# Output stores merged per tile and put on SyncE's queue, part of a weight block transposed in bf16, and a new order of all steps

## The chip, the core and the metric

The kernel runs on one core of one Trainium2 chip. The core has a matrix engine (TensorE, PE in the profile; its weight loads are shown as PEld), a vector engine (VectorE, DVE), a scalar engine (ScalarE, ACT), GpSimd (POOL) and SyncE (SP), each with its own queue of instructions that are carried out in order. SyncE does no arithmetic here, it issues transfers. ScalarE and GpSimd can issue transfers too. All transfers are moved by the same 16 DMA engines.

The metric is device time in microseconds of one execution.

## What is computed

A linear attention over 8 batches, 8 heads, 576 positions and 64 numbers per head, followed by a multiplicative feed-forward step on the 4608 tokens of width 512:

```python
phi(x) = where(x > 0, x, exp(x) - 1) + 1
kv  = einsum('bhsd,bhse->bhde', phi(k), v)
z   = sum(phi(k), axis=2)
num = einsum('bhsd,bhde->bhse', phi(q), kv)
den = einsum('bhsd,bhd->bhs', phi(q), z)[..., None] + 1e-06
x   = (num / den) with the heads side by side      # 4608 x 512
out = ((x @ w1) * (x @ w2)) @ w3 @ w_out           # w1, w2: 512 x 1024; w3: 1024 x 1024; w_out: 1024 x 512
```

Inputs and output are float32. The kernel forms w3 @ w_out once (it is called wf, 1024 x 512), so that each token needs x @ w1, x @ w2, their product, and one product with wf.

## The kernel before

**An order written out.** The program is the string ORDER, a list of steps such as `F.2.0` or `VC.3.0.v`. Each step is a small function `s_<kind>`; the letter at the end says which engine does its copy (a ScalarE, v VectorE, p GpSimd, s SyncE). The steps are recorded in this order, and each engine's queue holds its part of them in this order. An engine that waits at one instruction holds up all later ones of its queue.

**Loads.** All loads go through `load` (L150) on SyncE's queue into one of 13 buffers called `ld`: L3.i a block of 128 rows of w3, LO.x two blocks of w_out, LA.x and LB.x a quarter of w1 and w2 (256 columns), LQ/LK/LV.b.h half of q, k, v of batch b (576 KB). A load waits until the last reader of its buffer is done.

**The product wf.** T3.i transposes the eight 128 x 128 parts of block i of w3 in float32 on TensorE (L198) into a PSUM tile of two banks and copies it to bf16 (L201). CO casts w_out to bf16 (L179). FA.i (L209) and FB.i (L213) are four matmuls each of w3's block with w_out; FB copies the result to wf (L214). CA and CB cast the quarters of w1 and w2 (L183, L188).

**Attention.** EX is the exponential on ScalarE (L222), PT and PM are phi's other two parts on VectorE (L234, L241), VC casts v to bf16 (L244). KV.b.h is 36 small matmuls for half a batch's kv (L260) and a copy (L262). q is transposed on TensorE for batches 0 and 1 (QP, L273 and L274) and by a transposing transfer on SyncE's queue for the others (QD, L278). ND.t forms numerator and denominator of the 128 tokens of tile t (L292) and divides on VectorE (L298 to L300) into xn. A tile holds two sets of 64 tokens; a set is one batch b and one j of 9, with 64 tokens that stand 9 rows apart in the output, and tile t has sets 2t and 2t+1. Four tiles make a chunk of 512 tokens. xn is transposed on TensorE for chunks 0 and 1 (XP, L314 and L315) and by transposing transfers for the others, two tiles each (XD, L319).

**Feed-forward.** F.c.f is eight matmuls of 128 x 512 for chunk c and 128 columns f of w1 and w2 (L337), a copy of one product to SBUF on ScalarE (L343) and the multiplication on VectorE (L344). O.t is eight matmuls of the products with wf (L359) and a copy to o_sb (L366), which has five buffers. Four PSUM banks (`mm`) are shared by F, O, XP, FA and the warm-up; two tiles of two banks (`at`) by ND, KV, QP and T3.

**Stores.** S.t sends o_sb to HBM in two transfers of 64 rows on GpSimd's queue (L375). Q.35 is the last tile: two halves of 256 columns, each copied and stored on its own, on SyncE's and ScalarE's queues (L382, L385).

Of the kernel before, what the change touches and what calls it, by code (L numbers as in the profile page):

```python
# [14 lines left out]
P = 128  # L15
# [3 lines left out]


ORDER = """
L3.1 I.0 H.9 I.1 L3.0 T3.0.a T3.1.v LO.0 L3.2 T3.2.a CO.0.v LO.1 CO.1.v FA.1 FA.0 LO.2 CO.2.v FA.2
LO.3 CO.3.v FB.1.a L3.3 L3.5 FB.0.v L3.4 LQ.0.0 LQ.0.1 T3.3.v FB.2.v PT.q.0.1 PT.q.0.0 T3.4.a T3.5.a
EX.q.0.0 L3.6 LV.0.0 FA.3 PM.q.0.0 FA.4 EX.q.0.1 PM.q.0.1 FB.3.a I.2 T3.6.a LK.0.0 LK.0.1 VC.0.0.v
L3.7 LV.0.1 PT.k.0.0 EX.k.0.0 FA.5 LA.0 QP.0.1.v QP.0.0.a PM.k.0.0 EX.k.0.1 LQ.1.1 FB.4.a LB.0 FA.6
KV.0.0.a T3.7.a FB.5.a LA.3 PT.k.0.1 PM.k.0.1 LB.1 LA.1 VC.0.1.v KV.0.1.a ND.0 ND.1 CA.0.a FB.6.a
ND.2 XP.0.a LA.2 EX.q.1.1 ND.3 FA.7 XP.1.a XP.2.v XP.3.v FB.7.v CA.3.v CB.0.a PT.q.1.1 LK.1.0
PM.q.1.1 F.0.0 CB.1.v CA.1.a F.0.1 F.0.2 CA.2.a PT.k.1.0 LB.2 CB.2.v LQ.1.0 EX.k.1.0 PM.k.1.0 LB.3
LV.1.0 PT.q.1.0 F.0.3 F.0.4 EX.q.1.0 QP.1.1.v CB.3.a F.0.5 VC.1.0.a F.0.6 LK.1.1 PT.k.1.1 LV.1.1
EX.k.1.1 PM.k.1.1 KV.1.0.a PM.q.1.0 VC.1.1.a LQ.5.1 F.0.7 KV.1.1.a QP.1.0.a LQ.2.1 O.0.a LK.3.0 ND.4  # L30
ND.5 O.1.a LK.2.0 PT.k.2.0 EX.k.2.0 LV.2.0 XP.4.v XP.5.v EX.q.2.1 ND.6 ND.7 LK.2.1 O.2.v XP.6.a
EX.k.3.0 PT.k.3.0 XP.7.v VC.2.0.v LQ.2.0 PT.q.2.0 LV.3.0 LV.2.1 LQ.3.1 LV.4.1 LQ.3.0 PM.k.2.0 O.3.a
LK.4.1 EX.q.2.0 LK.4.0 PT.k.2.1 F.1.0 F.1.1 PT.q.2.1 PM.q.2.1 F.1.2 EX.k.2.1 PM.k.3.0 F.1.3 PT.q.3.1
# [25 lines left out]
def kernel(  # L59
# [61 lines left out]
    def at_tile(name):  # L121
        return take("at", name, [P, 2, 512], F32, name)
# [24 lines left out]
    def load(key, src, cols):  # L147
        t = raw[key] = take("ld", key, [P, HW], F32, key[0])[:, 0:cols]
        dst = t if len(src.shape) == 2 else t.rearrange("p (a x) -> p a x", a=src.shape[1])
        nc.sync.dma_start(out=dst, in_=src)  # L150
# [26 lines left out]

    def s_CO(x, e):
# [1 line left out]
        give("ld", ("wo", x))  # L180

    def s_CA(x, e):
        copy_of(e)(out=w1_sb[:, :, 256 * x:256 * x + 256],  # L183
                   in_=raw["wa", x].rearrange("p (c n) -> p c n", c=KC))
        give("ld", ("wa", x))

    def s_CB(x, e):
        copy_of(e)(out=w2_sb[:, :, 256 * x:256 * x + 256],  # L188
                   in_=raw["wb", x].rearrange("p (c n) -> p c n", c=KC))
        give("ld", ("wb", x))  # L190


    w3ts = {}

    def s_T3(i, e):
        tp = at_tile("w3p").rearrange("p a (c t) -> p (a c) t", t=P)
        for c in range(FC):
            nc.tensor.transpose(tp[:, c, :], raw["w3", i][:, c * P:(c + 1) * P], ident32)  # L198
# [12 lines left out]
    def s_FB(i, e):
        for c in range(4, 8):
            nc.tensor.matmul(wfs[i], w3ts[i][:, c, :], wo_sb[:, c, :], start=False, stop=(c == 7))  # L213
        copy_of(e)(out=wf_sb[:, i, :], in_=wfs[i])  # L214
        give("mm", ("wf", i))
# [35 lines left out]
    def s_KV(b, h, e):
        if h == 0:
            kvs[b] = take("kv", None, [P, 2, 2, E], BF16, "kv")
        kvp = at_tile("kvp")
        kh = by_set("k", phs["k", b, h])
        for j in range(J):
            for c in range(2):
                for u in range(2):
                    rows = slice(u * R, (u + 1) * R)
                    nc.tensor.matmul(kvp[c * R:(c + 1) * R, u, 0:E], kh[rows, c, j, :],  # L260
                                     vts[b % 2][rows, h, c, j, :], start=(j == 0), stop=(j == J - 1))
        copy_of(e)(out=kvs[b][:, h], in_=kvp[:, :, 0:E])  # L262
        give("at", "kvp")

    def q_tile(b, h):
# [100 lines left out]
        copy_of(e)(out=o_sbs[t], in_=o_ps)  # L366
# [59 lines left out]
```

## Time and profile before

| | |
|---|---|
| three executions | 259.6, 259.3 and 258.11 us, median 259.3 |
| the profiled execution | 259.34 us; its span from the first to the last instruction is 257.6 us |
| mean granted TensorE clock | 0.979 |
| TensorE busy | 235.3 us, 91% of the span |
| VectorE, ScalarE, GpSimd busy | 156.7 us, 116.2 us, 39.9 us |
| transfers | 55.79 MB, 217 GB/s on average |
| first F (F.0.0) starts | 36.75 us |
| last O's matmuls start | 249.75 us |

The matrix engine's busy time counts from the start of a matmul to its modelled end, so it does not say how fast the matmuls run; the granted clock does that. In a group of the profile, "x72 | 49.1, 686" means 72 instructions, 49.1 us in all, 686 ns each; what follows the next bar is the time that the engine stood idle ahead of them, and what ended it. "SPq" is SyncE's queue. A DMA share of 1.0 means that all 16 engines had packets all the time, and it can be above 1 where packets of two queues overlap.

### The profile page before, as it was taken

The page shows a single profiled execution, that of the slowest core. Times are in us where ns is not written, and L with a number is a line of the kernel's source. Part 1 is how long each engine was busy: PE and PEld are TensorE (multiplying, and loading weights), DVE is VectorE, ACT ScalarE, POOL GpSimd, SP SyncE. Part 2 cuts the span into 40 slices and gives each one's busy share as a digit, 9 for nine tenths or more (in the row PEclk, how much of TensorE's full clock was granted, in tenths as well). Part 3 has the DMA queues.
Part 4 walks back from the last instruction along what each step waited for, and adds up shares of the span by engine and source line. Part 5 has one row for each costly group of instructions (what it writes and reads, how often), then busy time and mean ns, then how long its engine had stood idle before and what let it go on. Part 6 is the DMA issues. An engine that isn't in the chain of part 4 may idle for free.

```text
span 257.6 us, 5461 instructions
## 1 busy us (share of the span) xinstructions
PE 235.3 (91%) x2206; PEld 114.2 (44%) x2229; DVE 156.7 (61%) x294; ACT 116.2 (45%) x165; POOL 39.9 (15%) x79
## 2 busy tenths in 40 slices
PE   6799689999999698999996999999999999999990
PEld 2465444454445343444443444444444444444450
DVE  0448588769898748897988359534557215424420
ACT  1328777957584247346555443235323232231310
POOL 2000000014101600050031101033201330132140
PEclk9999999999999979999999799999999999999996
DMA  6999999999999999799999923653714431331232
GB/s 246 394 401 396 368 356 370 390 390 403 400 267 288 331 320 299 146 204 233 370 187 267 294 45 59 160 106 83 150 43 83 91 73 41 81 84 25 57 85 78
DMA packets 52216, 55.79 MB, mean 217 GB/s; under 512 B 31264, under 2 KB 35616, under 8 KB 52192
## 3 DMA queue, kind: packets, MB, share of 16 engines
q1 hardware_dynamic: 48672, 46.15, 61.0%
q0 software_dynamic: 3360, 9.18, 14.0%
q8 instruction: 17, 0.28, 0.5%
q10 hardware_dynamic: 160, 0.13, 0.2%
q14 instruction: 7, 0.06, 0.1%
HBM read 38.80 MB, written 9.44 MB: 187 GB/s over the span
## 4 chain that ended last, share of the span: by engine, by line
PE 68%; DMA 17%; DVE 6%; SPq 3%; issue 2%; ACT 1%; DVEq 0%
PE a_ps L337 22%; PE b_ps L337 22%; PE o_ps L359 20%; DMA k<-in_k_dram 5%; DMA v<-in_v_dram 5%; DMA w<-in_moe_w_dram 4%; DMA q<-in_q_dram 3%; DVE xn L300 2%; PE nd L292 2%; SPq L150 2%; PE kvp L260 2%; DVE r L299 1%; SPq L278 1%; DVE phk L241 1%; DVE phk L234 1%
## 5 line engine op out<-in xcount | busy, mean ns | idle before, releaser
L337 PEld LDWEIGHTS <-w_sb 128*128 128x128 bf16 x576 | 55.9, 99 | 71.6 <-issue 5.6
L337 PE MATMUL a_ps<-xt,w_sb 128*128 128x512 bf16 x288 | 75.8, 386 | 2.3 <-DMA xt<-xn 2.3
L344 DVE TENSOR_TENSOR ab<-a_sb,b_ps 128x512 bf16<-128x512 f32 x72 | 49.1, 686 | 47.0 <-PE b_ps L337 43.2
L337 PE MATMUL b_ps<-xt,w_sb 128*128 128x512 bf16 x288 | 75.4, 385 | 1.2 <-DVE ab L344 1.2
L343 ACT COPY a_sb<-a_ps 128x512 f32<-128x512 f32 x72 | 42.0, 584 | 68.1 <-PE a_ps L337 67.7
L375 POOL DMA_DIRECT2D out_dram<-o_sb x70 | 38.6, 556 | 210.4 <-ACT o_sb L366 109.8
L359 PE MATMUL o_ps<-wf_sb,ab 128*128 128x512 bf16 (+1 forms) x278 | 64.7, 373 | 1.1 <-issue 0.2
L359 PEld LDWEIGHTS <-ab 128*128 128x128 bf16 x296 | 28.1, 98 | 31.2
L366 ACT COPY o_sb<-o_ps 128x512 f32<-128x512 f32 x19 | 11.1, 585 | 34.2 <-PE o_ps L359 34.2
L300 DVE TENSOR_TENSOR xn<-nd,r 128x512 bf16<-128x512 f32 x36 | 24.9, 692 | 1.2
L222 ACT ACTIVATE ek<-k 128x1152 bf16<-128x1152 f32 x16 | 18.7, 1167 | 8.0 <-DMA k<-in_k_dram 8.0
L222 ACT ACTIVATE eq<-q 128x1152 bf16<-128x1152 f32 x16 | 18.4, 1162 | 3.5 <-DMA q<-in_q_dram 2.5
L366 DVE COPY o_sb<-o_ps 128x512 f32<-128x512 f32 x16 | 10.9, 688 | 13.8 <-PE o_ps L359 13.8
L234 DVE TENSOR_SCALAR phq<-q 128x1152 bf16<-128x1152 f32 x16 | 12.0, 754 | 3.4 <-DMA q<-in_q_dram 3.4
L234 DVE TENSOR_SCALAR phk<-k 128x1152 bf16<-128x1152 f32 x16 | 12.1, 753 | 2.8 <-DMA k<-in_k_dram 2.8
L241 DVE TENSOR_TENSOR phk<-phk,ek 128x1152 bf16<-128x1152 bf16 x16 | 11.9, 751 | 0.6 <-ACT ek L222 0.5
L241 DVE TENSOR_TENSOR phq<-phq,eq 128x1152 bf16<-128x1152 bf16 x16 | 12.0, 754 | 0.4
L198 PE MATMUL w3p<-ident,w 128*128 128x128 f32 x64 | 8.1, 274 | 3.5 <-DMA w<-in_moe_w_dram 2.3
L201 ACT CAST w3t<-w3p 128x1024 bf16<-128x1024 f32 x6 | 6.0, 1014 | 11.3 <-PE w3p L198 11.3
L298 DVE TENSOR_SCALAR r<-nd 128x8 f32<-128x8 f32 x36 | 5.7, 159 | 8.1 <-PE nd L292 8.1
L292 PE MATMUL nd<-kv,qt 64*64 64x65 bf16 x576 | 9.4, 195 | 1.3 <-DVE xn L300 0.4
L292 PEld LDWEIGHTS <-qt 64*64 64x64 bf16 x576 | 7.1, 108 | 7.1 <-issue 5.4
(42 smaller groups left out, 111.8 us busy)
## 6 DMA issues: line engine op xcount, KB each, us to landing
q<-in_q_dram SPq DMA_DIRECT2D x16, 576.0 KB, 10.8
v<-in_v_dram SPq DMA_DIRECT2D x16, 576.0 KB, 11.1
k<-in_k_dram SPq DMA_DIRECT2D x16, 576.0 KB, 8.6
out_dram<-o_sb POOLq DMA_DIRECT2D x70, 128.0 KB, 3.2
w<-in_moe_w_dram SPq DMA_DIRECT2D x8, 512.0 KB, 10.2
wo<-in_moe_w_out_dram SPq DMA_DIRECT2D x4, 512.0 KB, 7.7
wa<-in_moe_w_dram SPq DMA_DIRECT2D x4, 512.0 KB, 9.8
wb<-in_moe_w_dram SPq DMA_DIRECT2D x4, 512.0 KB, 10.2
```

The lines of the kernel that those rows point to most:

```text
L198: nc.tensor.transpose(tp[:, c, :], raw["w3", i][:, c * P:(c + 1) * P], ident32)
L222: nc.scalar.activation(out=t, in_=raw[n, b, h], func=AF.Exp)
L234: nc.vector.tensor_scalar(out=by_set(n, t), in0=by_set("k", raw[n, b, h]), scalar1=0.0, scalar2=1.0, op0=ALU.max, op1=ALU.add)
L241: nc.vector.tensor_tensor(out=t, in0=t, in1=by_set("k", es[n, b, h]), op=ALU.min)
L292: nc.tensor.matmul(nd[g * R:(g + 1) * R, c, (2 * h + u) * E:(2 * h + u + 1) * E], qts[b, h][rows, j, u * R:(u + 1) * R], kvs[b][rows, h, u ...
L300: nc.vector.tensor_tensor(out=xns[c0][:, m].rearrange("p (c a x) -> p c a x", c=2, x=D), in0=n4[:, :, :, 0:D], in1=r.unsqueeze(3).to_broad ...
L337: nc.tensor.matmul(ops_[c0, f][i], w[:, w_row(kc), f * P:(f + 1) * P], xts[c0][:, :, kc, :], start=(kc == 0), stop=(kc == KC - 1))
L343: nc.scalar.copy(out=a_sb, in_=a_ps)
L344: nc.vector.tensor_mul(out=abs_[c0][:, f, :], in0=a_sb, in1=b_ps)
L359: nc.tensor.matmul(o_ps, abs_[c0][:, f, m * P:(m + 1) * P], wf_sb[:, f, cols], start=(f == 0), stop=(f == FC - 1))
L366: copy_of(e)(out=o_sbs[t], in_=o_ps)
L375: {"p": nc.gpsimd, "s": nc.sync}[e].dma_start(out=out_rows(t, g), in_=o_sbs[t][g * R:(g + 1) * R, :])
```

## The change

- **Stores.** `out_rows` and the two transfers of S.t are replaced by `store`. Where both sets of a tile belong to one batch (31 of the tiles 0 to 34), one transfer of 128 rows is issued, whose output pattern is 2 x 64 x 512. In tiles 4, 13, 22 and 31 the sets belong to two batches, and two transfers of 64 rows remain. All S are on SyncE's queue now; GpSimd issues no transfer. Q.35's two halves use `store` too.
- **w3.** T3 and the matmuls are cut into smaller steps: T3.i.0 and T3.i.1 (four transposes and a copy each), FW.i.0 to FW.i.3 (two matmuls each, the copy with the last). For blocks 3, 4, 5, 6 and 7 a step C3.i first casts the block to bf16, and the transposes run in bf16. Block 0 is loaded in two halves of columns (LH.0.0, LH.0.1).
- **w1 and w2.** Parts 2 and 3 are now two row blocks each of columns 512 to 1023, rather than 256 columns of all rows.
- **kv.** For batches 2 to 7, KV.b.0 and KV.b.1 become KB.b: 72 matmuls into one PSUM tile and one copy.
- **The order** is another throughout. More VC and O copies are ScalarE's (13 of 16 and 20 of 35, before 8 and 19).

```diff
 ORDER = """
-L3.1 I.0 H.9 I.1 L3.0 T3.0.a T3.1.v LO.0 L3.2 T3.2.a CO.0.v LO.1 CO.1.v FA.1 FA.0 LO.2 CO.2.v FA.2
...
-LV.3.1 PM.q.2.0 QD.2.0 VC.3.0.v QD.2.1 F.1.4 LV.5.0 EX.q.3.1 PM.k.2.1 KV.2.0.v VC.2.1.a LK.3.1 S.0.p
-ND.8 F.1.5 F.1.6 LK.5.0 PM.q.3.1 EX.k.4.0 F.1.7 KV.2.1.a EX.q.3.0 KV.3.0.a S.1.p S.2.p EX.k.3.1
-PT.q.3.0 ND.9 O.4.v ND.10 ND.11 XD.2.0 PM.q.3.0 LQ.4.1 O.5.a O.6.a XD.2.1 QD.3.1 S.3.p O.7.a
...
-F.8.4 F.8.5 S.30.p S.31.p F.8.6 F.8.7 O.32.v O.33.v O.34.a Q.35 S.32.p S.33.p S.34.p
+LO.1 L3.1 I.0 LO.0 CO.0.a L3.2 H.9 L3.6 LO.2 I.1 T3.1.0.a T3.1.1.a FW.1.0.v C3.6.v T3.2.0.a T3.2.1.v
...
+PT.q.3.0 PM.q.3.0 F.1.5 F.1.6 ND.8 KB.2.a F.1.7 QD.2.0 QD.2.1 QD.3.1 VC.3.0.a EX.k.3.0 ND.9 QD.3.0
+XD.2.0 ND.10 O.4.a ND.11 PM.k.3.0 XD.2.1 VC.3.1.a PT.q.4.0 EX.k.3.1 S.0.s S.1.s PT.k.3.1 PM.k.3.1
+S.2.s LK.4.0 O.5.v O.6.a O.7.a LQ.4.1 LK.5.0 F.2.0 F.2.1 F.2.2 LV.4.0 S.3.s EX.k.4.1 KB.3.a ND.12
...
+F.8.5 F.8.6 O.31.v F.8.7 O.32.a O.33.v O.34.a S.31.s S.32.s S.33.s S.34.s Q.35
 """
...
+    def s_LH(i, x, e):
+        cols = slice(x * NCH, (x + 1) * NCH)
+        if x == 0:
+            raw["w3", i] = take("ld", ("w3", i), [P, HW], F32, "w3")[:, 0:DFF]
+        nc.sync.dma_start(out=raw["w3", i][:, cols], in_=moe_w3[i * P:(i + 1) * P, cols])
...
+    def w_part(w, x):
+        return w[:, :, 256 * x:256 * x + 256] if x < 2 else w[:, 2 * x - 4:2 * x - 2, NCH:DFF]
...
-    def s_T3(i, e):
-        tp = at_tile("w3p").rearrange("p a (c t) -> p (a c) t", t=P)
-        for c in range(FC):
-            nc.tensor.transpose(tp[:, c, :], raw["w3", i][:, c * P:(c + 1) * P], ident32)
+    def s_C3(i, e):
+        t = w3bs[i] = take("a_sb", None, [P, DFF], BF16, "w3b")
+        copy_of(e)(out=t, in_=raw["w3", i])
         give("ld", ("w3", i))
...
+    def s_T3(i, x, e):
+        if x == 0:
+            w3ps[i] = at_tile("w3p", ("w3p", i))
+            w3ts[i] = take("w3t", None, [P, FC, P], BF16, "w3t")
+        src, idt = (w3bs[i], ident) if i in w3bs else (raw["w3", i], ident32)
...
+        for c in range(4):
+            nc.tensor.transpose(tp[:, c, :], src[:, (4 * x + c) * P:(4 * x + c + 1) * P], idt)
+        copy_of(e)(out=w3ts[i][:, 4 * x:4 * x + 4], in_=tp)
...
-    def s_FA(i, e):
...
-    def s_FB(i, e):
...
+    def s_FW(i, x, e):
+        if x == 0:
+            wfs[i] = mm_tile("wf_ps", ("wf", i))
+        for c in (2 * x, 2 * x + 1):
+            nc.tensor.matmul(wfs[i], w3ts[i][:, c, :], wo_sb[:, c, :], start=(c == 0), stop=(c == FC - 1))
+        if x == 3:
+            copy_of(e)(out=wf_sb[:, i, :], in_=wfs[i])
+            give("mm", ("wf", i))
...
+    def s_KB(b, e):
+        kvs[b] = take("kv", None, [P, 2, 2, E], BF16, "kv")
+        kvp = at_tile("kvp")[:, :, 0:2 * E].rearrange("p u (h x) -> p h u x", h=2)
+        for h in range(2):
+            kv_mm(kvp[:, h], b, h)
+        copy_of(e)(out=kvs[b], in_=kvp)
         give("at", "kvp")
...
-    def out_rows(t, g):
-        b, j = divmod(2 * t + g, J)
-        return out[b * S:(b + 1) * S, :].rearrange("(p j) n -> p j n", j=J)[:, j, :]
+    def store(queue, t, o_sb, cols):
+
+        (b, j), (b1, j1) = divmod(2 * t, J), divmod(2 * t + 1, J)
+        rows = out.rearrange("(b p j) n -> j b p n", b=B, j=J)
+        if b == b1:
+            queue.dma_start(out=rows[j:j + 2, b, :, cols],
+                            in_=o_sb[:, cols])
+        else:
+            queue.dma_start(out=rows[j, b, :, cols], in_=o_sb[0:R, cols])
+            queue.dma_start(out=rows[j1, b1, :, cols], in_=o_sb[R:P, cols])
 
     def s_S(t, e):
-        for g in range(2):
-            {"p": nc.gpsimd, "s": nc.sync}[e].dma_start(
-                out=out_rows(t, g), in_=o_sbs[t][g * R:(g + 1) * R, :])
+        store({"p": nc.gpsimd, "s": nc.sync}[e], t, o_sbs[t], slice(0, DM))
...
-            for g in range(2):
-                queue.dma_start(out=out_rows(t, g)[:, cols], in_=o_sb[g * R:(g + 1) * R, cols])
+            store(queue, t, o_sb, cols)
```

More of the change, by code (lines that the diff above doesn't have):

```diff
@@ L119, in copy_of, with at_tile @@
         return {"a": nc.scalar.copy, "v": nc.vector.tensor_copy, "p": nc.gpsimd.tensor_copy}[e]
[L121 to L122 removed]
+    def at_tile(name, key=None):
+        return take("at", key or name, [P, 2, 512], F32, name)
     def mm_tile(name, key=None):
@@ L182, in s_CA @@
     def s_CA(x, e):
-        copy_of(e)(out=w1_sb[:, :, 256 * x:256 * x + 256],
-                   in_=raw["wa", x].rearrange("p (c n) -> p c n", c=KC))
+        copy_of(e)(out=w_part(w1_sb, x),
+                   in_=raw["wa", x].rearrange("p (c n) -> p c n", c=KC if x < 2 else 2))
         give("ld", ("wa", x))
     def s_CB(x, e):
-        copy_of(e)(out=w2_sb[:, :, 256 * x:256 * x + 256],
-                   in_=raw["wb", x].rearrange("p (c n) -> p c n", c=KC))
+        copy_of(e)(out=w_part(w2_sb, x),
+                   in_=raw["wb", x].rearrange("p (c n) -> p c n", c=KC if x < 2 else 2))
@@ L190, in s_CB @@
         give("ld", ("wb", x))
     w3ts = {}
-    def s_T3(i, e):
-        tp = at_tile("w3p").rearrange("p a (c t) -> p (a c) t", t=P)
-        for c in range(FC):
-            nc.tensor.transpose(tp[:, c, :], raw["w3", i][:, c * P:(c + 1) * P], ident32)
+    w3bs = {}
+    def s_C3(i, e):
+        t = w3bs[i] = take("a_sb", None, [P, DFF], BF16, "w3b")
+        copy_of(e)(out=t, in_=raw["w3", i])
         give("ld", ("w3", i))
-        t = w3ts[i] = take("w3t", None, [P, FC, P], BF16, "w3t")
-        copy_of(e)(out=t, in_=tp)
-        give("at", "w3p")
@@ L204 @@
-    wfs = {}
-    def s_FA(i, e):
-        wfs[i] = mm_tile("wf_ps", ("wf", i))
-        for c in range(4):
-            nc.tensor.matmul(wfs[i], w3ts[i][:, c, :], wo_sb[:, c, :], start=(c == 0), stop=False)
-    def s_FB(i, e):
[L212 to L215, printed above, removed]
+    w3ps = {}
+    def s_T3(i, x, e):
[3 more added lines that the diff above has]
+        src, idt = (w3bs[i], ident) if i in w3bs else (raw["w3", i], ident32)
+        tp = w3ps[i][:, x]
+        if i in w3bs:
+            tp = tp.bitcast(BF16)[:, 0:NCH]
+        tp = tp.rearrange("p (c t) -> p c t", t=P)
+        for c in range(4):
+            nc.tensor.transpose(tp[:, c, :], src[:, (4 * x + c) * P:(4 * x + c + 1) * P], idt)
+        copy_of(e)(out=w3ts[i][:, 4 * x:4 * x + 4], in_=tp)
+        if x == 1:
+            give("at", ("w3p", i))
+            if i not in w3bs:
+                give("ld", ("w3", i))
@@ L249, with kv_mm @@
     kvs, qts, xns, xts = {}, {}, {}, {}
[L251 to L254, printed above, removed]
+    def kv_mm(kvp, b, h):
         kh = by_set("k", phs["k", b, h])
@@ L259, in s_KV @@
                     rows = slice(u * R, (u + 1) * R)
-                    nc.tensor.matmul(kvp[c * R:(c + 1) * R, u, 0:E], kh[rows, c, j, :],
+                    nc.tensor.matmul(kvp[c * R:(c + 1) * R, u, :], kh[rows, c, j, :],
                                      vts[b % 2][rows, h, c, j, :], start=(j == 0), stop=(j == J - 1))
-        copy_of(e)(out=kvs[b][:, h], in_=kvp[:, :, 0:E])
+    def s_KV(b, h, e):
+        if h == 0:
+            kvs[b] = take("kv", None, [P, 2, 2, E], BF16, "kv")
+        kvp = at_tile("kvp")[:, :, 0:E]
+        kv_mm(kvp, b, h)
+        copy_of(e)(out=kvs[b][:, h], in_=kvp)
+        give("at", "kvp")
+    def s_KB(b, e):
+        kvs[b] = take("kv", None, [P, 2, 2, E], BF16, "kv")
+        kvp = at_tile("kvp")[:, :, 0:2 * E].rearrange("p u (h x) -> p h u x", h=2)
+        for h in range(2):
+            kv_mm(kvp[:, h], b, h)
+        copy_of(e)(out=kvs[b], in_=kvp)
         give("at", "kvp")
```

63 lines of the change are left out of this document (33 added, 30 removed).

## The prediction

> **What bounds the kernel now.** I read the span in forty slices first, then the chain that ended last, then the busy times in windows, then the timeline at the dips, then the transfers. In the slices:
>
> ```profile
> PE   6799689999999698999996999999999999999990
> PEclk9999999999999979999999799999999999999996
> DMA  6999999999999999799999923653714431331232
> GB/s 246 394 401 396 368 356 370 390 390 403 400 267 288 331 320 299 146 204 233 370 187 267 294 45 59 160 106 83 150 43 83 91 73 41 81 84 25 57 85 78
> ```
>
> Both TensorE and the DMA engines are full up to about 150 us; from there TensorE alone is, and the DMA engines stand at a third of their time. The chain says the same, with TensorE at two thirds:
>
> ```profile
> PE 68%; DMA 17%; DVE 6%; SPq 3%; issue 2%; ACT 1%; DVEq 0%
> ```
>
> Where TensorE loses time is seen in windows of 10 us (busy time per engine, granted clock, mean DMA share, GB/s):
>
> ```profile
> 80.00:90.00 10.00, 7.70 (x115) 3.67 (x114) 7.73 (x18) 2.98 (x5) 5.02 (x8) 0.99 1.15 315
> 90.00:100.00 10.00, 8.81 (x35) 3.56 (x33) 6.56 (x10) 4.53 (x7) 0.00 (x0) 0.84 1.09 286
> 130.00:140.00 10.00, 8.35 (x116) 3.81 (x117) 9.33 (x20) 4.17 (x6) 2.22 (x4) 1.00 1.05 228
> 140.00:150.00 10.00, 9.34 (x86) 4.28 (x86) 4.82 (x9) 5.23 (x8) 2.06 (x4) 0.83 1.07 270
> 240.00:250.00 10.00, 9.95 (x52) 5.03 (x52) 3.50 (x6) 1.92 (x4) 2.12 (x5) 1.00 0.21 48
> ```
>
> And what each dip is, in the timeline of TensorE (start, length, idle before it):
>
> ```profile
> 88.91 1.11 PE L337 MATMUL a_ps<-xt,w_sb 128*128 128x512 bf16 x4 [2.25 <-DMA xt<-xn]
> 89.81 1.91 PE L337 MATMUL b_ps<-xt,w_sb 128*128 128x512 bf16 x4
> 91.52 1.84 PE L337 MATMUL a_ps<-xt,w_sb 128*128 128x512 bf16 x4
> 93.19 1.03 PE L337 MATMUL b_ps<-xt,w_sb 128*128 128x512 bf16 x4
> ...
> 140.66 0.55 PE L260 MATMUL kvp<-vt,phk 64*64 64x65 bf16 x36 [2.20 <-ACT vt L244]
> ...
> 141.37 1.89 PE L337 MATMUL a_ps<-xt,w_sb 128*128 128x512 bf16 x4
> 143.05 1.68 PE L337 MATMUL b_ps<-xt,w_sb 128*128 128x512 bf16 x4
> ```
>
> F.2.0 waits 2.25 us for a transposed xt, and eight matmuls behind it then run slow: (1.91 - 1.03) + (1.84 - 1.03) = 1.7 us, in the window with clock 0.84. The second wait costs 2.20 us, and (1.89 - 1.03) + (1.68 - 1.03) = 1.5 us in the window with clock 0.83. Together 7.6 us are there to be won between F.0.0 and the end. Behind 150 us there is nothing.
>
> **The w3 part, kv and the copies.** F.0.0 starts here, behind the last load that it needs, v of batch 0:
>
> ```profile
> 29.37 0.76 DVE L244 CAST vt<-v 128x1152 bf16<-128x1152 f32 x1 [1.16 <-DMA v<-in_v_dram]
> ...
> 36.75 1.03 PE L337 MATMUL a_ps<-xt,w_sb 128*128 128x512 bf16 x4
> ```
>
> Before, that load was the 18th, behind 9.24 MB; now L3.7 and half of w3's block 0 come after it, 0.79 MB less. The rate to divide by is that of 20 to 60 us:
>
> ```profile
> DMA packets 9131, 15.15 MB, mean 379 GB/s; under 512 B 421, under 2 KB 4517, under 8 KB 9126
> q1 hardware_dynamic: 9118, 15.05, 105.6%
> ```
>
> 0.79 MB at 379 GB/s is 2.1 us. Half of it is lost again, since CA.0, XP.1 and XP.2 now stand on VectorE among ND.0 to ND.3: F.0.0 comes 1 us earlier. The bf16 transposes:
>
> ```profile
> L198 PE MATMUL w3p<-ident,w 128*128 128x128 f32 x64 | 8.1, 274 | 3.5 <-DMA w<-in_moe_w_dram 2.3 <-ACT wf_sb L214 1.2
> L183 ACT CAST w_sb<-wa 128x1024 bf16<-128x1024 f32 x3 | 3.1, 1048 | 0.0
> L273 PE MATMUL qp<-ident,phq 128*128 128x128 bf16 x36 | 2.5, 219 | 0.2 <-DVE phq L241 0.2
> L183 DVE CAST w_sb<-wa 128x1024 bf16<-128x1024 f32 x1 | 0.7, 682 | 0.0
> ```
>
> Forty transposes go from 8.1/64 = 0.127 us to about 2.5/36 = 0.069 us, 2.3 us of TensorE, and are paid for with five casts, four on ScalarE (1.05 us) and one on VectorE (0.68 us). All that lies ahead of F.0.0, where the loads decide: nothing on the path, and if that cover were gone, 2.3 us less. One copy of kv per batch in place of two takes six copies away, but KB now needs both halves of k and v: from -1 to +1 us, nothing taken. The halves of w1 and w2 keep their bytes; nothing.
>
> **The order between F.1.7 and F.2.0.** Now ND.11, then O.5, O.6 and O.7 stand ahead of F.2.0, and no load stands on SyncE's queue between the q transposes and XD.2.1 (before, one did):
>
> ```profile
> 81.37 1.46 SPq L150 DMA_DIRECT2D q<-in_q_dram  x1
> 83.28 1.35 SPq L319 DMA_TRANSPOSE xt<-xn  x1
> ```
>
> That alone would bring back between nothing and the 7.6 us; I take half, 4 us. Up to here the change would give 259.3 - 1 - 4 = 254 us, and 251 to 259 by its bounds.
>
> **The stores.** S.t was two transfers of 64 rows from GpSimd's queue, each with an output pattern of 64 rows of 512 numbers. Now 31 of the 35 tiles go out in one transfer on SyncE's queue whose output pattern is 2 x 64 rows: the two sets are 512 numbers apart and the rows 4608, so these two dimensions can't be joined into one of 128, and the outermost one counts 2. The input's counts 128. How a transfer is dealt to the engines, the trace shows at one place, Q.35's two stores on ScalarE's queue:
>
> ```profile
> q10 hardware_dynamic: 160, 0.13, 0.2%
> ```
>
> 160 packets for two transfers of 64 rows are 80 each: 64 rows and 16 more, one for each engine, so four rows an engine. That fits a transfer cut into equal shares along its outermost dimension. Cut along one that counts 2, the store would give two shares, and two engines would carry the 256 KB, 128 KB each. Every transfer of the trace before leads with 64 or 128, so it shows neither this nor the contrary. The Trainium skill (DMA: Bandwidth & Descriptors, Why a DMA increments its semaphore by 16 and not by 1) states it as a rule: the number of engines is the largest up to 16 that divides the slowest dimension of both patterns, here 2. By that rule the sum is the one that follows; without it the 254 us above stand. No run here shows it yet.
>
> What it costs is worked out from three windows: 88 to 150 us, 200 to 250 us, and the one above.
>
> ```profile
> q1 hardware_dynamic: 20181, 13.37, 90.0%
> ...
> q<-in_q_dram SPq DMA_DIRECT2D x6, 576.0 KB, 7.2
> k<-in_k_dram SPq DMA_DIRECT2D x5, 576.0 KB, 6.8
> v<-in_v_dram SPq DMA_DIRECT2D x5, 576.0 KB, 6.6
> ...
> qt<-phq SPq DMA_TRANSPOSE x8, 7.3
> xt<-xn SPq DMA_TRANSPOSE x6, 5.1
> ...
> q0 software_dynamic: 993, 2.75, 24.2%
> ...
> out_dram<-o_sb POOLq DMA_DIRECT2D x23, 128.0 KB, 2.2
> ```
>
> A store on all engines at the load rate is 0.262 MB / 379 GB/s = 0.69 us; on two engines eight times that, 5.5 us. That is the fast end: each engine gets 64 rows on end, as in a stream of loads. The slow end is the stores' own busy time, 24.2% of 50 us for 2.75 MB, 4.4 us per MB, so 1.15 us and on two engines 9.2 us. I take 5.5, since those short stores carry four rows an engine and their ends weigh heavily.
>
> These two engines also carry their sixteenth of all else. The first S now stands behind XD.2.1, which was issued at 83.28 us, and with the earlier front at about 82. Behind it in the new order lie 22 loads of 0.59 MB, 13.0 MB at 379 GB/s = 34 us, and 20 transposes. One transpose: 90% of 62 us is 55.8 us, less 16 loads (9.44 MB at 105.6% of 40 us per 15.05 MB, 2.8 us per MB, 26.5 us), so 29.3 us for 14, or 2.1 each; twenty are 42 us. The 31 merged stores and Q.35, as much as one, are 32 x 5.5 = 176 us; the eight unmerged halves 3. Sum: 82 + 34 + 42 + 176 + 3 = 337 us, 2.2 us for the last landing, and 1.7 us between span and time (259.34 less 257.6): **341 us**, against 259.3 for the profiled execution and a median of 259.3. TensorE's work doesn't hide it. From the chain, one output tile and half of an F step:
>
> ```profile
> 61.31 1.73 PE o_ps L359 x8
> 63.04 0.86 PE a_ps L337 x4
> ```
>
> A chunk of four tiles is eight F of 1.73 us and four O of 1.73: 20.8 us, 5.2 us per tile, where the two engines need 5.5 us for its store alone.
>
> What is queued behind: S waits for its copy, and loads and transposes wait behind S in one queue; o_sb has five buffers, so O.5's copy waits for S.0's landing, TensorE waits for the PSUM bank of O.5 and then stands in step with the stores. The stall thus moves from xt to o_sb.
>
> Bounds of this case: with loads and transposes overlapping by the 1.15 of the window above, 76 us become 66, and at 5.0 us a store 160: 82 + 66 + 160 + 3 = 311 us; at 7 us, halfway to the slow end, 389 and some waiting of the queue: 305 to 405.
>
> **The rivals.**
> - The stores spread over all engines (the 64 rows inside the outer 2 are cut, four rows an engine). Then the queue carries 0.69 us per tile, nothing beside TensorE's 5.2 us, and the front and half of the dips come back: 254 us, 251 if both dips go wholly. For it: the q10 row, if the cut is along the rows and not the outermost dimension.
> - The stores spread, but VectorE becomes the bound. Between F.0.4 and F.1.0 the order now has one PT, two PM and two O copies more on VectorE:
>
> ```profile
> L234 DVE TENSOR_SCALAR phk<-k 128x1152 bf16<-128x1152 f32 x16 | 12.1, 753 | 2.8 <-DMA k<-in_k_dram 2.8
> L366 DVE COPY o_sb<-o_ps 128x512 f32<-128x512 f32 x16 | 10.9, 688 | 13.8 <-PE o_ps L359 13.8
> ```
>
> Three of 0.75 us (PM as PT) and two of 0.69 are 3.6 us, and if TensorE waits for them the clock falls as it did twice, 1.7: 259.3 + 3.6 + 1.7 = 264.6 us, with neither dip won back. It decides where F.1.0's product comes over 2.2 us behind its matmuls. Against it: the front is 1 us earlier, and VC and kv copies went to ScalarE.
> - Two engines at the slow end, 9.2 us: 82 + 76 + 294 + 3 + 4 = 459 us. For it: that is what the trace's only stores show. Against it: their four rows an engine.
>
> **How the numbers follow.** Two engines carry the merged stores: 0.74, of which 0.62 lie in 305 to 405 us, 0.04 below, 0.08 above. Spread and faster: 0.18. Spread and late VectorE: 0.08, of which 0.03 end within 0.5% of before, which is about what a measurement of this kernel can tell from no change. So faster 0.18, same 0.03, slower 0.79. The range that leaves at most 2 in 10 out goes from 250 us, into the first rival, to 405 us.
>
> **What would show it.** In the changed profile: merged stores that land after 8 us or more rather than the 2.2 of before; a mean DMA share that stays near 3 tenths for the last third while TensorE has gaps of some us ahead of o_ps or a_ps, with waits put down to the o_sb copies or the stores; granted clock below 0.9; o_sb copies that wait on out_dram transfers. Fewer than 16 closing packets per store would be the plainest sign. Stores that land in 3 us, with TensorE at 9.95 of 10 behind 150 us, would make it wrong at the outermost dimension; a time above 405 us would make it wrong at the 5.5 us.

## The result, and the profile after

| | before | after |
|---|---|---|
| median of four executions | 259.45 us (258.11 to 261.3) | 334.67 us (333.38 to 335.62) |
| ratio, 95% interval | | 1.289 [1.2798, 1.2981] |
| profiled execution, its span | 259.34 us, 257.6 us | 334.51 us, 332.7 us |
| mean granted clock | 0.979 | 0.900 |
| first F starts | 36.75 us | 40.28 us |
| last matmul ends | 250.8 us | 312.6 us |
| from there to the end of the span | 6.8 us | 20.1 us |

The changed kernel is 29% slower. Ratios here compare only executions in the faster of two states, since a kernel's executions can differ by some per cent from one state to the other. The 75.1 us between the two spans lie 3.5 ahead of the first F, 58.3 between it and the last matmul (272.3 against 214.0 us), and 13.3 behind that. The slices of after:

```profile
PE   6798899999726994299995669839769994599500
PEclk9999999999955999589999599969979999599955
DMA  7999999965345739769779936961894119212111
GB/s 283 398 392 371 380 391 390 389 160 108 82 160 202 256 112 72 144 225 192 197 237 128 167 68 192 67 142 34 112 66 105 56 52 66 64 51 72 33 50 42
```

One slice is 8.3 us. TensorE has holes from the eleventh slice on, at 83 us, and the granted clock falls to half in seven slices, the last two of them without a matmul. The DMA row is near full to 66 us, drops ahead of the first store, and doesn't come back: the rate goes from 390 GB/s to 82 and is never again above 256, where before it was 331 at 87 us and 370 at 125. At the end TensorE stands still for two slices while transfers go on at 1 tenth. The chain of waits of after:

```profile
PE 54%; DMA 28%; DVE 6%; SPq 2%; ACT 2%; issue 2%; DVEq 0%; ACTq 0%
```

28% of 332.7 us is 93 us of transfers on the path, where it was 17% of 257.6 us, 44 us. The waits of after that bear on the stores, and the largest ones of TensorE (in all, times, longest):

```profile
...
ACT o_sb L406 <- DMA out_dram<-o_sb: 37.5, 5, 13.4
...
PE a_ps L377 <- DMA xt<-xn: 21.9, 4, 10.7
...
PE nd L332 <- DMA qt<-phq: 8.8, 2, 6.7
PE b_ps L377 <- ACT o_sb L406: 7.6, 3, 3.3
DVE o_sb L406 <- DMA out_dram<-o_sb: 6.8, 1, 6.8
```

The o_sb copies wait for stores, and TensorE waits for those copies, and for the transposes xt and qt, which stand among the stores in SyncE's queue. How many engines carry a store is read from Q.35 in the table of queues (packets, MB, share):

```profile
q1 hardware_dynamic: 52432, 55.32, 68.7%
...
q10 hardware_dynamic: 130, 0.13, 0.1%
```

q10 holds one store now, 128 rows of 256 columns: 130 packets, which are 128 rows and 2 that close it. Before there were two of 64 rows with 160, four rows and one closing packet for each of 16 engines. The share agrees. In windows of after, at 90 us and in the last third:

```profile
90.00:100.00 10.00, 2.06 (x5) 0.65 (x5) 0.69 (x1) 0.59 (x1) 0.00 (x0) 0.62 0.44 147
...
260.00:270.00 10.00, 10.00 (x77) 4.55 (x76) 1.56 (x4) 3.42 (x6) 0.00 (x0) 1.00 0.13 52
310.00:320.00 10.00, 2.61 (x21) 1.76 (x18) 0.42 (x1) 0.96 (x2) 0.00 (x0) 0.88 0.13 46
320.00:333.00 13.00, 0.00 (x0) 0.00 (x0) 0.00 (x0) 0.00 (x0) 0.00 (x0) 0.50 0.12 44
```

With nothing but stores under way, the share is 0.12 to 0.13, and two engines of 16 are 0.125. They move 44 to 52 GB/s together, so 262 KB take 5.0 to 6.0 us. This is the rule that the prediction named from the Trainium skill (DMA: Bandwidth & Descriptors, Why a DMA increments its semaphore by 16 and not by 1), the largest number up to 16 that divides the slowest dimension of both patterns; 130 packets and 0.125 agree with its 2.

What a store takes is read from the engines that stand in step with it. TensorE at the first stores:

```profile
88.36 1.03 PE L377 MATMUL a_ps<-xt,w_sb 128*128 128x512 bf16 x4
94.79 1.87 PE L377 MATMUL b_ps<-xt,w_sb 128*128 128x512 bf16 x4 [5.40 <-DVE o_sb L406]
...
99.80 1.86 PE L377 MATMUL a_ps<-xt,w_sb 128*128 128x512 bf16 x4 [3.15 <-ACT o_sb L406]
...
104.92 1.86 PE L377 MATMUL b_ps<-xt,w_sb 128*128 128x512 bf16 x4 [3.26 <-ACT o_sb L406]
```

and the two copies on ScalarE that released the last two:

```profile
99.17 0.59 ACT L406 COPY o_sb<-o_ps 128x512 f32<-128x512 f32 x1 [13.44 <-DMA out_dram<-o_sb]
104.29 0.59 ACT L406 COPY o_sb<-o_ps 128x512 f32<-128x512 f32 x1 [4.54 <-DMA out_dram<-o_sb]
```

The copies start as stores land, 104.29 - 99.17 = 5.12 us apart. The single packets in the trace say the same: at the end of the span two packets of 2 KB, one stored row each, are under way at a time, and two start every 0.080 us, so that 64 rows for each of two engines take 5.1 us. TensorE follows them, 5.01 and 5.12 us from one wait to the next: four matmuls at half speed take 1.9 us of it, the rest is waiting.

### The profile page after: what moved, and what is told of

Read it like the earlier page. It is cut to its first block, busy times and chain, and to the rows that moved or that the text cites. A ratio compares the mean times of both kernels' runs of the same rounds, so it can differ in the third digit from the quotient of the medians.

```text
span 332.7 us, 5427 instructions
## 1 busy us (share of the span) xinstructions
PE 251.3 (76%) x2229; PEld 116.8 (35%) x2229; DVE 156.3 (47%) x296; ACT 121.2 (36%) x170; POOL 1.3 (0%) x9
## 3 DMA queue, kind: packets, MB, share of 16 engines
q1 hardware_dynamic: 52432, 55.32, 68.7%
## 4 chain that ended last, share of the span: by engine, by line
PE 54%; DMA 28%; DVE 6%; SPq 2%; ACT 2%; issue 2%; DVEq 0%; ACTq 0%
PE b_ps L377 17%; PE a_ps L377 17%; DMA xt<-xn 11%; PE o_ps L399 11%; DMA out_dram<-o_sb 8%; DMA v<-in_v_dram 5%; PE wf_ps L241 4%; DMA qt<-phq 3%; PE w3p L228 2%; DVE xn L340 2%; DMA wo<-in_moe_w_out_dram 2%; SPq L359 2%; DVE ab L384 1%; PE nd L332 1%; PE kvp L286 1%
## 5 line engine op out<-in xcount | busy, mean ns | idle before, releaser
L377 PEld LDWEIGHTS <-w_sb 128*128 128x128 bf16 x576 | 57.3, 102 | 118.8 <-issue 55.9
L377 PE MATMUL a_ps<-xt,w_sb 128*128 128x512 bf16 x288 | 79.3, 400 | 25.1 <-DMA xt<-xn 21.9
L377 PE MATMUL b_ps<-xt,w_sb 128*128 128x512 bf16 x288 | 79.6, 402 | 18.5 <-ACT o_sb L406 7.6
L399 PE MATMUL o_ps<-wf_sb,ab 128*128 128x512 bf16 (+1 forms) x296 | 69.1, 388 | 0.2 <-DVE ab L384 0.2
L399 PEld LDWEIGHTS <-ab 128*128 128x128 bf16 x296 | 29.1, 101 | 35.0 <-issue 4.7
L406 ACT COPY o_sb<-o_ps 128x512 f32<-128x512 f32 x20 | 11.7, 586 | 67.8 <-DMA out_dram<-o_sb 37.5
L241 PE MATMUL wf_ps<-wo_sb,w3t 128*128 128x512 bf16 x64 | 17.6, 409 | 0.0
L273 ACT CAST vt<-v 128x1152 bf16<-128x1152 f32 x13 | 15.0, 1155 | 0.6 <-DMA v<-in_v_dram 0.6
L228 PE MATMUL w3p<-ident,w 128*128 128x128 f32 x24 | 5.6, 377 | 3.4 <-ACT w3t L229 2.9
```

The costliest lines, as they stand in the source:

```text
L273: copy_of(e)(out=vts[b % 2][:, h, :, :, 0:D], in_=raw["v", b, h].rearrange("p (c j d) -> p c j d", c=2, j=J))
L377: nc.tensor.matmul(ops_[c0, f][i], w[:, w_row(kc), f * P:(f + 1) * P], xts[c0][:, :, kc, :], start=(kc == 0), stop=(kc == KC - 1))
L399: nc.tensor.matmul(o_ps, abs_[c0][:, f, m * P:(m + 1) * P], wf_sb[:, f, cols], start=(f == 0), stop=(f == FC - 1))
```

## The experiments

Eight kernels beside these two. The kernel before had medians of 259.9 to 261.1 us on their chips; ratios are against it.

**The stores in two transfers again.** All else of the change is kept, the queue too.

```diff
-        if b == b1:
-            queue.dma_start(out=rows[j:j + 2, b, :, cols],
-                            in_=o_sb[:, cols])
-        else:
-            queue.dma_start(out=rows[j, b, :, cols], in_=o_sb[0:R, cols])
-            queue.dma_start(out=rows[j1, b1, :, cols], in_=o_sb[R:P, cols])
+        queue.dma_start(out=rows[j, b, :, cols], in_=o_sb[0:R, cols])
+        queue.dma_start(out=rows[j1, b1, :, cols], in_=o_sb[R:P, cols])
```

> The changed kernel with each store as two transfers of 64 rows again, still on SyncE's queue, and the same order; nothing else differs. Theory (a store whose output pattern leads with 2 is carried by two DMA engines, and the stores set the pace): the time falls by 70 us or more, to 254 to 264 us, stores land in 3 to 4 us, no copy to o_sb waits for a store. Rival (the stores are slow because they share SyncE's queue with loads and transposes, merged or not): it stays above 310 us. Second rival (the new order as such is slow): it stays above 280 us with waits put down to VectorE or loads.

254.13 us (253.39 to 254.87), ratio 0.9776 [0.9708, 0.9844]: 80 us below after, by this one edit, and inside the expected range. Its rate, its queues and its stores (packets, MB, share; then issues, KB, us to landing):

```profile
GB/s 255 393 403 390 368 377 387 392 388 390 293 109 77 142 189 402 370 194 256 393 178 161 269 318 211 270 4 129 98 136 127 143 66 118 68 97 25 26 79 129
...
q1 hardware_dynamic: 53392, 55.32, 74.1%
...
q10 hardware_dynamic: 160, 0.13, 0.2%
...
out_dram<-o_sb SPq DMA_DIRECT2D x70, 128.0 KB, 2.4
```

The rate falls from the eleventh slice of 6.3 us here too, so this drop is the new order's and not the stores'; but at 95 us it is back at 402. SyncE's queue has 53392 - 52432 = 960 packets more than in after. That is 30 for each of 32 stores (31 tiles and Q.35's half): 32 closing packets rather than 2. So every merged store ran on two engines, not only Q.35's. The expectation that no o_sb copy waits for a store was too strong: five do, for 10.6 us in all, but TensorE hardly feels it. The dips of before are gone: from F.2.0 on, these are TensorE's waits for o_sb copies, the last of them its longest wait for anything:

```profile
91.69 1.02 PE L377 MATMUL b_ps<-xt,w_sb 128*128 128x512 bf16 x4 [0.19 <-DVE o_sb L406]
...
94.19 1.02 PE L377 MATMUL b_ps<-xt,w_sb 128*128 128x512 bf16 x4 [0.35 <-ACT o_sb L406]
...
193.57 1.02 PE L377 MATMUL b_ps<-xt,w_sb 128*128 128x512 bf16 x4 [0.64 <-ACT o_sb L406]
```

**The merged stores in the old kernel.** Before, with `store` of after and every `S.t.p` turned to `S.t.s` at its old place.

```diff
-LV.3.1 PM.q.2.0 QD.2.0 VC.3.0.v QD.2.1 F.1.4 LV.5.0 EX.q.3.1 PM.k.2.1 KV.2.0.v VC.2.1.a LK.3.1 S.0.p
+LV.3.1 PM.q.2.0 QD.2.0 VC.3.0.v QD.2.1 F.1.4 LV.5.0 EX.q.3.1 PM.k.2.1 KV.2.0.v VC.2.1.a LK.3.1 S.0.s
...
+        store({"p": nc.gpsimd, "s": nc.sync}[e], t, o_sbs[t], slice(0, DM))
```

> The kernel before with the store part alone: merged stores on SyncE's queue, in the places where its order had them. Theory: 315 to 345 us, copies to o_sb that wait for stores some 5 us apart, a tail of 15 us or more behind the last matmul. Rival (the new order is at fault): below 275 us.

338.14 us (337.12 to 339.17), ratio 1.3021 [1.2897, 1.3145], clock 0.872. With the old order, front and kv the same loss appears, so the store part alone makes it. The signs are the expected ones: two o_sb copies that wait for stores start 5.11 us apart (95.20 and 100.31), and the span ends 24.4 us behind the last matmul. The edit both merges the stores and moves them to SyncE's queue; what the queue has in it is a later experiment's.

**The merged stores on GpSimd's queue.** After, with every `S.t.s` turned to `S.t.p`; Q.35 stays.

```diff
-XD.2.0 ND.10 O.4.a ND.11 PM.k.3.0 XD.2.1 VC.3.1.a PT.q.4.0 EX.k.3.1 S.0.s S.1.s PT.k.3.1 PM.k.3.1
+XD.2.0 ND.10 O.4.a ND.11 PM.k.3.0 XD.2.1 VC.3.1.a PT.q.4.0 EX.k.3.1 S.0.p S.1.p PT.k.3.1 PM.k.3.1
```

> The changed kernel with its merged stores on GpSimd's queue instead of SyncE's, same order. Theory: a merged store is still carried by two engines and takes some 5 us, but if GpSimd's queue deals its pairs out in turn, no pair of engines is full, and it ends between 255 and 275 us; if the same two engines carry all of them, 310 us or more as before. Rival (the queue is the cause): 250 to 262 us and stores that land in 3 us.

303.36 us (299.66 and 307.06): between the expectations, so all of them missed. Its rows of the stores:

```profile
q0 software_dynamic: 16752, 9.29, 14.6%
...
out_dram<-o_sb POOLq DMA_DIRECT2D x31, 256.0 KB, 11.7
```

That SyncE's queue is the cause falls: without a store on it, but for Q.35's half, even the execution of 299.66 us is 45 us slower than the split version, and a merged store lands after 11.7 us. The packets are more than on SyncE's queue: 16752 = 8 x 48 + 31 x 528, 528 for each merged store rather than 130. Their sizes in the trace tell what they are: 64 of 4096 bytes, which are the 256 KB, 16 of 4 bytes that close the transfer, and 448 of 8 bytes. Where one merged store is alone under way, two of the 4096-byte packets are under way at once for 4 to 6 of its 6 to 7 us, and more than two for 0.2 us at most; where several stores are, there are often four and more. That reads as two engines for a merged store on this queue as well, and other engines for the next one. The 448 are as many as 32 for each of the other fourteen engines; the trace doesn't name the engine of a packet, so this stays a reading of the counts.

The stall is in another place here. No o_sb copy waits for a store, and TensorE's largest waits are for transposes: 17.4 us for qt and 8.2 for xt, though no store but Q.35's half stands in their queue. What holds the transposes up was not tried.

**The split stores on GpSimd's queue.** The last edit and the first together.

```diff
-XD.2.0 ND.10 O.4.a ND.11 PM.k.3.0 XD.2.1 VC.3.1.a PT.q.4.0 EX.k.3.1 S.0.s S.1.s PT.k.3.1 PM.k.3.1
+XD.2.0 ND.10 O.4.a ND.11 PM.k.3.0 XD.2.1 VC.3.1.a PT.q.4.0 EX.k.3.1 S.0.p S.1.p PT.k.3.1 PM.k.3.1
...
-        if b == b1:
-            queue.dma_start(out=rows[j:j + 2, b, :, cols],
-                            in_=o_sb[:, cols])
-        else:
-            queue.dma_start(out=rows[j, b, :, cols], in_=o_sb[0:R, cols])
-            queue.dma_start(out=rows[j1, b1, :, cols], in_=o_sb[R:P, cols])
+        queue.dma_start(out=rows[j, b, :, cols], in_=o_sb[0:R, cols])
+        queue.dma_start(out=rows[j1, b1, :, cols], in_=o_sb[R:P, cols])
```

> The changed kernel with the stores exactly as before the change (two transfers of 64 rows, GpSimd's queue), so the new order, the bf16 blocks, KB and the w1 and w2 parts alone. If the front is worth what it lost in the changed profile (F.0.0 3.5 us later, F.1.0 2.4 us later) and the dips at F.2.0 and F.5 are gone: 254 to 259 us. If the dips stay: 260 to 264 us. Against the run on SyncE's queue it tells what the queue alone does: within 3 us by the theory.

256.85 us (254.02 to 258.83), ratio 0.981 [0.9718, 0.9903], inside the range expected if the dips are gone. Its interval overlaps that of the split stores on SyncE's queue: with split stores, the queue is worth at most a few us in the new order.

**The queue alone, in the old kernel.** Before, with `S.t.p` turned to `S.t.s` at the old places, the stores split as they were.

```diff
-ND.8 F.1.5 F.1.6 LK.5.0 PM.q.3.1 EX.k.4.0 F.1.7 KV.2.1.a EX.q.3.0 KV.3.0.a S.1.p S.2.p EX.k.3.1
+ND.8 F.1.5 F.1.6 LK.5.0 PM.q.3.1 EX.k.4.0 F.1.7 KV.2.1.a EX.q.3.0 KV.3.0.a S.1.s S.2.s EX.k.3.1
```

> The kernel before with its 70 stores of 64 rows on SyncE's queue instead of GpSimd's, in the places of its own order, and nothing else. Theory (the queue costs little where the stores use all engines, but S waits in line with loads): 256 to 264 us, nowhere near 300. Rival (sharing the queue is itself a large cost): above 275 us.

266.7 us (265.99 to 268.48), ratio 1.0328 [1.0259, 1.0397], 2.7 us above the theory's range. TensorE's two dips of before grew:

```profile
92.79 1.89 PE L337 MATMUL a_ps<-xt,w_sb 128*128 128x512 bf16 x4 [5.21 <-DMA xt<-xn]
...
147.86 0.71 PE L260 MATMUL kvp<-vt,phk 64*64 64x65 bf16 x36 [5.02 <-ACT vt L244]
```

from 2.25 and 2.20 us to 5.21 and 5.02. A store waits in its queue until its copy is there, and the loads and transposes behind it wait too: SyncE's queue stands 25.7 us in all at stores whose copy isn't done. That this is what makes the dips longer is argued from the order of the queue. In the old order the queue costs 7 to 9 us (by the medians and by the ratio); in the new order nothing that can be told, by the two kernels with split stores.

**Every fourth store merged.** After, with eight merged stores rather than 31 (tiles 0, 8, 12 and so on to 32), Q.35 split.

```diff
-        if b == b1:
+        if b == b1 and t % 4 == 0:
```

> The changed kernel with merged stores on SyncE's queue in tiles 0, 8, 12, 16, 20, 24, 28 and 32 alone; the others, and Q.35, as two transfers of 64 rows. Theory (two engines that are full set the pace: 32 stores of some 5.1 us and the two engines' share of all else exceed what TensorE needs): eight of them are 41 us in 165 us of stores, the two engines are not full, o_sb's five buffers take the longer landing up, and the time is 252 to 260 us. Rival (each merged store costs a fixed wait of its own, (334.7 - 254.1) / 32 = 2.5 us): 274 us.

263.29 us (260.77 to 265.74, ten executions), ratio 1.0101 [1.0055, 1.0147]: between the two expectations. TensorE at the first merged store, then windows there and late:

```profile
96.76 1.87 PE L377 MATMUL b_ps<-xt,w_sb 128*128 128x512 bf16 x4 [5.25 <-DVE o_sb L406]
98.42 1.86 PE L377 MATMUL a_ps<-xt,w_sb 128*128 128x512 bf16 x4
```

```profile
90.00:100.00 10.00, 4.75 (x16) 1.75 (x14) 1.38 (x2) 1.66 (x3) 0.00 (x0) 0.83 0.82 242
...
240.00:250.00 10.00, 10.00 (x48) 4.55 (x47) 4.13 (x6) 2.50 (x5) 0.00 (x0) 1.00 0.19 43
```

The two profiled executions, this one and the fully split version's, have spans of 262.3 and 253.1 us, 9.2 apart. From F.0.0 to the last matmul it is 6.9 us, and that is S.0: 5.25 us of waiting for o_sb, and eight matmuls at half speed, 1.7 us. The other 2.3 us stand behind the last matmul, 6.4 us to the end of the span rather than 4.0. There S.32 is a merged store, and Q.35's second transfer on ScalarE's queue is issued 3.0 us behind its first, not 0.6; that the one causes the other was not tried. In between no wait of TensorE is over 0.7 us: the merged stores there have at least three split tiles between them and hide. So a merged store hasn't a fixed price. The readings fit a price that is paid where the two engines get work faster than 5.1 us per store, or where a buffer or the end of the kernel waits for one.

**The cast behind the copies.** The version with split stores on SyncE's queue; CO.0, the cast of w_out's first block, goes from ahead of w3's first transposed copy on ScalarE to behind it, on VectorE.

```diff
-LO.1 L3.1 I.0 LO.0 CO.0.a L3.2 H.9 L3.6 LO.2 I.1 T3.1.0.a T3.1.1.a FW.1.0.v C3.6.v T3.2.0.a T3.2.1.v
+LO.1 L3.1 I.0 LO.0 L3.2 H.9 L3.6 LO.2 I.1 T3.1.0.a T3.1.1.a CO.0.v FW.1.0.v C3.6.v T3.2.0.a T3.2.1.v
```

> The changed kernel with split stores on SyncE's queue, and one step moved: CO.0 from ahead of T3.1.0 on ScalarE's queue to behind T3.1.1 on VectorE's. Theory (ScalarE waits in CO.0 for the third load while a transposed block is ready, TensorE stands still 3 us and its clock falls): the wait of ScalarE for wo goes from 6 us to under 2, the granted clock of 10 to 20 us from 0.59 to over 0.9, and F.0.0 comes 1 to 3 us earlier, 251 to 253.5 us. Rival (the front hangs on the loads): no change of F.0.0, 254 us.

251.1 us (249.03 to 252.95), ratio 0.9738 [0.9663, 0.9813], inside the theory's range. In the time this isn't a gain that can be told from nothing: the split version's ratio is 0.9776 [0.9708, 0.9844], measured on another chip. What the edit does is seen in the profile. The start of the split version with CO.0 in its old place, first ScalarE, then TensorE:

```profile
7.98 1.04 ACT L192 CAST wo_sb<-wo 128x1024 bf16<-128x1024 f32 x1 [5.96 <-DMA wo<-in_moe_w_out_dram]
8.93 0.58 ACT L229 CAST w3t<-w3p 128x512 bf16<-128x512 f32 x1
```

```profile
5.68 0.63 PE L228 MATMUL w3p<-ident,w 128*128 128x128 f32 x4 [0.78 <-DMA w<-in_moe_w_dram]
9.57 1.11 PE L228 MATMUL w3p<-ident,w 128*128 128x128 f32 x4 [3.26 <-ACT w3t L229]
...
42.40 1.03 PE L377 MATMUL a_ps<-xt,w_sb 128*128 128x512 bf16 x4
```

and with CO.0 behind:

```profile
6.50 0.59 ACT L229 CAST w3t<-w3p 128x512 bf16<-128x512 f32 x1 [4.49 <-PE w3p L228]
```

```profile
7.14 0.65 PE L228 MATMUL w3p<-ident,w 128*128 128x128 f32 x4 [0.68 <-ACT w3t L229]
...
36.12 1.03 PE L377 MATMUL a_ps<-xt,w_sb 128*128 128x512 bf16 x4
```

The copy of w3 stood behind a cast that waited for the third load. TensorE waited 3.26 us for that copy and then ran at half speed: four transposes took 1.11 us, not 0.65. The windows from 10 to 20 us show the clock, 0.59 with CO.0 ahead and 1.00 with it behind:

```profile
10.00:20.00 10.00, 8.81 (x40) 5.03 (x39) 3.01 (x5) 5.61 (x8) 0.00 (x0) 0.59 1.04 402
```

```profile
10.00:20.00 10.00, 8.75 (x66) 4.89 (x65) 6.54 (x13) 6.65 (x8) 0.00 (x0) 1.00 1.04 402
```

40 matmuls ran in that window in the one and 66 in the other, and F.0.0 starts 6.3 us earlier, more than the 1 to 3 us expected. The second four transposes start 2.4 us earlier; by 21 us, behind the stretch at half speed, it is 5.0. The rest comes just ahead of F.0.0: in the split version the granted clock is 0.50 from 38.6 to 42.0 us as well, for a reason that was not looked for. The medians differ by 3.0 us only, as the profiled executions are the slowest of the split version's (254.87) and the fastest of this one's (249.03).

**The old front with the new rest.** Before's functions and order up to F.0.0; from there after's order (but for the loads and casts of w1 and w2 that before has behind F.0.0), KB, and split stores on SyncE's queue. The lines are the starts of after's order and of this one's.

```diff
-LO.1 L3.1 I.0 LO.0 CO.0.a L3.2 H.9 L3.6 LO.2 I.1 T3.1.0.a T3.1.1.a FW.1.0.v C3.6.v T3.2.0.a T3.2.1.v
...
+L3.1 I.0 H.9 I.1 L3.0 T3.0.a T3.1.v LO.0 L3.2 T3.2.a CO.0.v LO.1 CO.1.v FA.1 FA.0 LO.2
...
```

> The stretch up to F.0.0 as in the kernel before (float32 transposes of all eight blocks, its loads and quarters of w1 and w2), from F.0.0 on the order of the changed kernel with KB, stores as two transfers of 64 rows on SyncE's queue. Theory (the new front is what costs F.0.0 its 3.5 to 6 us, and everything behind it is bound by TensorE): F.0.0 at 37 us or so, and 5 us less than the run with split stores on SyncE's queue, 247 to 251 us. Rival (the lost front is made up for by loads that have come further, so that it costs nothing): 253 to 256 us.

252.27 us (251.88 to 253.94), ratio 0.9766 [0.9716, 0.9817], 1.3 us above the expected range, and by the ratio level with the split version, as the rival had it. F.0.0 starts at 37.11 us, 5.3 earlier than in the split version with the new front, but part of that is given back at once:

```profile
44.79 1.02 PE L343 MATMUL a_ps<-xt,w_sb 128*128 128x512 bf16 x4 [1.83 <-ACT a_sb L349]
```

Ahead of that copy on ScalarE stand two casts of w1 and w2, CA.1 and CB.2; that they are what delays it was not tried. The new front in itself (bf16 transposes, halves, other order) shows no gain over the old one, and with CO.0 moved one of 1.2 us in the medians, which these intervals don't tell from nothing.

## Why the prediction was right, and where it was off

**The stores: right, in mechanism and nearly in size.** The step was that a store whose output pattern leads with 2 is cut into two shares for two engines. 130 packets, 960 packets of difference and a share of 0.125 show it; undoing it alone brings back 80 us, and doing it alone costs 78 us. The price was taken as 5.5 us, from the load rate; measured 5.1, where copies stand in step with stores and in the spacing of the packets. The first store was put at 82 us and is issued at 85.7:

```profile
85.74 4.84 SPq L414 DMA_DIRECT2D out_dram<-o_sb  x3
```

With these two in its sum: 85.7 + 34 + 42 + 32 x 5.1 + 3 + 2.2 + 1.7 = 332 us, against 334.51 in the profiled execution. So the terms were off by -13 and +4 us, and the forecast of 341 by 6. The 34 and 42 us for loads and transposes were not measured alone. Of the 247 us from 85.7 to the end, packets of stored rows are under way in 171, near the 163 + 3 of the sum; the other 76 are as much as 34 + 42, but in 11.5 of them nothing is under way, and loads and transposes also run beside stores. So that these two terms come out is in part luck.

**Where the stall went: half right.** The step was "The stall thus moves from xt to o_sb". It does appear at o_sb: 37.5 us on ScalarE and 6.8 on VectorE are waits of copies for stores, and TensorE waits 16.1 us for such copies. But it didn't leave xt: TensorE waits 21.9 us for xt, where it was 2.3 before, and 8.8 for qt. The prediction named transposes as queued behind stores, but didn't count them as a place of the stall. Whether the queue or the two engines hold them is open; with the merged stores on GpSimd's queue TensorE still waited 25.6 us for them.

**The slow end, 9.2 us, fell.** Its argument was the stores' own busy time with four rows an engine; on two engines each has 64 rows on end. The price per byte was the loads', as the row nearest to it said.

**The dips: the size was off.** Half of 7.6 us was taken. In the split version F.0.0 to the last matmul takes 206.6 us, 7.4 less than before, and no wait or clock of the two dips is left there, so nearly all came back. Another 2.8 us, which the prediction didn't have, came at the end: 4.0 us from the last matmul to the end of the span rather than 6.8.

**The front: wrong.** The step was "F.0.0 comes 1 us earlier", from 2.1 us of loads less and half of it lost on VectorE. F.0.0 came 3.5 us later in after and 5.65 later in the split version, whose front is the same code. The step treated all work ahead of F.0.0 as hidden behind loads. What it missed is one instruction's place: CO.0 waits on ScalarE for the third load, and w3's first copy behind it holds TensorE. The clock at the start has a part in it that isn't explained: in after the first four transposes took 1.09 us already, half speed, ahead of that wait, and in the split version 0.63. With CO.0 moved, F.0.0 starts at 36.12 us. Before's front has it at 36.75 to 38.37 in the profiled executions of four kernels that use it, so the step's 1 us, without that wait, is neither shown nor refuted. The same holds for the bf16 transposes: no gain on the path was seen, as the prediction had it, but they were not tried alone.

**The rivals.** Spread stores with 254 us: refuted for merged stores by the packets. Its number is the time of the split version, 254.1, but by luck, as errors cancel: against its terms the front was 6.7 us worse, the dips 3.4 and the end 2.8 better. VectorE as the bound: not seen; from F.0.0 to F.1.0 it is 25.2 us in after (40.28 to 65.46) and 26.1 in before (36.75 to 62.88). The sign "stores that land after 8 us" could not be read, as the table of transfers of after gives no landing for them; the copies' distance did in its place. The other signs were there: closing packets, the share (0.26 from 260 to 330 us), the waits of o_sb; the clock of 0.900 in the profiled execution is at the edge of "below 0.9", and the other three have 0.87 to 0.895.

## What to carry to other kernels

Ask of each transfer what the outermost dimension of both of its patterns counts: on SyncE's queue a store of 2 x 64 rows took two engines and 5.1 us, where two stores of 64 rows took sixteen each, and joining transfers is no saving where it costs engines. A slow transfer hurts by the rate at which its engines are given work, and by the buffers that wait for it: eight such stores spread out cost 8 to 9 us, thirty-one and Q.35 80. And a load that is "hidden" still sets the start, if an instruction that waits for it stands ahead of one that TensorE waits for.

## What was not expected of the hardware

- On GpSimd's queue a merged store is 528 packets rather than 130: the 64 of 4 KB that carry the data, for the most part two under way at a time, 16 of 4 bytes, and 448 of 8 bytes. It landed after 11.7 us, and the kernel took 303 us rather than 335.
- Waits of TensorE of 2 to 3 us can be enough to slow the matmuls behind them to half speed for some us: 2.25 us at F.2.0 before, and 3.26 us at the start of the split version, with a clock of 0.59 from 10 to 20 us. They need not: in after a wait of 3.23 us was followed by matmuls at full speed, so the length of one wait doesn't decide it.

```profile
200.21 1.04 PE L377 MATMUL a_ps<-xt,w_sb 128*128 128x512 bf16 x4 [3.23 <-DMA xt<-xn]
```

- A window can show a granted clock of 1.00 where none was recorded. In after, the second four float32 transposes take 1.12 us, as long as at half speed, in a stretch that says 1.00:

```profile
9.04 1.12 PE L228 MATMUL w3p<-ident,w 128*128 128x128 f32 x4 [2.19 <-ACT w3t L229]
```

```profile
10.00:20.00 10.00, 8.78 (x39) 4.81 (x38) 3.66 (x7) 6.13 (x8) 0.00 (x0) 1.00 1.04 402
```

39 matmuls in 8.78 us of busy time, against 66 in 8.75 with CO.0 behind, say the same as the duration. The clock records of this trace begin at 17.3 us, those of the split version at 4.5. So at the start of a run the durations are the surer sign.
